# Sums for a blocked matrix product, shared out anew between GpSimd and VectorE: attention, then a bilinear feed-forward layer, on one Trainium2 core

## The chip, the cores and the metric

The kernel runs on one core of one Trainium2 chip. The core has five engines that run at the same time, each with its own queue of instructions: TensorE (PE in the profile; PEld are its weight loads), VectorE (DVE), ScalarE (ACT), GpSimd (POOL) and SyncE (SP, which here only starts DMA transfers). They share a large on-chip memory, SBUF; the results of products land in a smaller one, PSUM, which GpSimd doesn't read here. Semaphores tell an engine that another has done its part. The metric is the device time of one launch, in microseconds (us); less is better.

## What is computed

Four batches of 8 heads, 768 positions and 64 numbers a head go through block attention: a small 8 x 8 matrix P per head, normalized by rows and columns five times, mixes the 8 blocks of k and v, and each block of q attends to its mixed block. The result, as x with 3072 rows of 512, goes through a feed-forward layer that multiplies two projections by each other.

```python
def _attn_ref(q, k, v, sort_net):
    ...
    k_sorted = np.einsum('bhij,bhjcd->bhicd', P, k_b).reshape(B, H, S, D)
    v_sorted = np.einsum('bhij,bhjcd->bhicd', P, v_b).reshape(B, H, S, D)
    ...
    scores = scale * np.matmul(q_b, k_sb.transpose(0, 1, 2, 4, 3))
    ...
    return np.matmul(attn, v_sb).reshape(B, H, S, D).astype(np.float32)

def _moe_ref(x, w_a, w_b, w_out):        # x: 3072 x 512
    a = x @ w_a                          # w_a, w_b: 512 x 1536
    b = x @ w_b
    return (a * b @ w_out).astype(np.float32)   # w_out: 1536 x 512
```

## The kernel before, in words

Everything is computed in bf16 with fp32 sums. The work goes batch by batch: while TensorE runs the feed-forward layer of batch b, the attention of batch b + 1 is put between its steps. The order on every engine is written out by hand: `interleave` (L697) runs a list of feed-forward steps and, after the step numbers given in `places`, the units of the next batch's attention. Each engine takes its instructions strictly in that order.

**Attention units** (`units_full`, L672). For pair g of heads: M mixes the blocks of k and v on TensorE and ScalarE copies them out; R computes the scores (`pair_scores`, L326) into tiles `sc` in PSUM, and ScalarE takes their exponent; O (`pair_o` and `one_o`, L341 and L273) multiplies by v into tiles `o_ps`, and VectorE divides by the sums (`rec` at L282, `xp` at L284). The tiles `mix`, `sc` and `o_ps` come from one pool of two PSUM buffers (`psA`): a new one waits until the one before last has been read. Then DMA transposes on SP's queue bring x to its place (`xT`). M also has GpSimd's share: for pairs 5 and 7 it spreads P over a tile `s_all` (L167, one half of the heads of a later batch each time), and regroups q and k, v (`pair_q`, `regroup`). On GpSimd's queue lie the loads of later pairs too, with a one-element copy `held` (L295) ahead of some of them, which waits until x of an earlier pair has landed.

**Feed-forward steps.** `ffn_ab` (L391) computes one block of 128 columns of a and of b for half of the 768 rows: 4 products of 384 columns each into a tile `pf` of a pool of four PSUM buffers (`psF`). ScalarE copies a out (L403), and VectorE multiplies it with b straight from PSUM (L404) into `hT`, the product h. When the columns of h that belong together are done, sums of them are due.

**Why there are sums.** The products with w_out (`ffn_out_pair`, L491), and in batch 3 those with w_a (`ab_four`, L592), treat rows and columns as 2 x 2 blocks and need seven block products instead of eight, but sums and differences of blocks as operands. There are four kinds:

- `weight_sum` (L451): five sums `w_sums[n]` of blocks of w_out, each in two pieces of 128 x 768, made once;
- `h_sums` (L460): for each block of columns m, one sum of two parts (768 elements), one of one part (384) and a difference in place (768);
- `a_sum` (L558) and `x_sum` (L573): the same for w_a and for x, for batch 3 alone.

Sums that are due stand in the list `sums_due`; `some_sums(n)` (L383) puts the next n of them on VectorE's queue, after a step of `ffn_ab`, in `ffn_out` and in `ab_four`; `sums_for` (L387) puts those there that a product is about to need. The ten pieces of `weight_sum` become due in the eighth step of batch 0's second half (L853), when the loads of w_out (L127) have been started.

**The outputs of batch 0.** For the first third of the columns, `ffn_out` (L422) uses plain products, for c = 0 and then c = 3, each in two parts with `some_sums(2)` after each; the rest goes through `ffn_out_pair` in four parts: parts 1 and 2 need the w_sums n = 1, 2 and 0, and parts 3 and 4 need n = 4 and 3. The units of batch 1's attention stand between these parts.

**Batch 3** (`ab_four`). One row m of it makes four blocks of h: 7 block products of two matmuls each for a, 4 products of four matmuls each for b, 30 matmuls of 384 columns in all. ScalarE copies two of the products out (L622, L624), and GpSimd adds them to y (L625); VectorE adds a third (L628). The blocks h(1, 0) and h(0, 1) come from `middle` (ScalarE's copy of a, L618) times `kept_b` (ScalarE's copy of b to SBUF, L613), multiplied on GpSimd (L632, L636). The corners h(0, 0) and h(1, 1) take y less a product (L642), and VectorE multiplies them with b from PSUM (L645). Six rows follow each other, then the w_out products of batch 3 and the last stores. The x sums of batch 3 are made on VectorE after the last two parts of batch 2's outputs (L884, L885).

Of the kernel before, what the change touches and what calls it, by code (L numbers as in the profile page):

```python
# [9 lines left out]
FP32 = mybir.dt.float32  # L10
# [3 lines left out]
ALU = mybir.AluOpType  # L14
# [9 lines left out]
def kernel(  # L24
# [11 lines left out]
    nc = tc.nc  # L36
    P = 128
# [14 lines left out]
    KH = KO // 2  # L52
# [8 lines left out]
    HW = S // 2  # L61
# [6 lines left out]
    ld = ctx.enter_context(tc.tile_pool(name="ld", bufs=4))  # L68
# [311 lines left out]
    sums_due = []  # L380
    PACE = (1,1,1,1,1,1,1,2,2,2,2,3)

    def some_sums(n):  # L383
        for _ in range(min(n, len(sums_due))):
            sums_due.pop(0)[1]()
# [36 lines left out]
    def ffn_out(b, c):  # L422
        v = {}

        def mms(ms):
            for m in ms:
                nc.tensor.matmul(v["po"], lhsT=hTs[b][:, m, c * P:(c + 1) * P],
                                 rhs=w_out_sb[:, m, :], start=(m == 0), stop=(m == KO - 1))

        def part1():  # L430
            v["po"] = psF.tile([P, DMODEL], FP32, tag="F", name="po")
            mms(range(KH))
            some_sums(2)

        def part2():
            mms(range(KH, KO))
            o_sb = outp.tile([P, DMODEL], FP32, tag="o2", name="o_sb", bufs=3)
            copy("act", o_sb, v["po"])
            store(b, c, o_sb)
            some_sums(2)  # L440

        return [part1, part2]
# [5 lines left out]
    sums = {}  # L448
    w_sums = [const.tile([P, KH, NH], BF16, name=f"w_sum{n}") for n in range(5)]

    def weight_sum(n, m, nm):  # L451
        x, y = (B11, B12, B21, B11, B21)[n], (B22, B22, B11, B12, B22)[n]
        return n, lambda: nc.vector.tensor_tensor(
            out=w_sums[n][:, m:m + nm], in0=x[:, m:m + nm], in1=y[:, m:m + nm],
            op=ALU.subtract if n in (1, 2) else ALU.add)

    def h_part(b, r, c, m):
        return hTs[b][:, c * KH + m, r * HW:(r + 1) * HW]

    def h_sums(b, m, nm):  # L460
        n0, n = (P, HW - P) if b == 0 else (0, HW)
        if b not in sums:
            sums[b] = ffp.tile([P, KH, 3, HW], BF16, tag="hs", name="hs")
        hT, hs = hTs[b], sums[b]

        def h(r, c, step):
            return _ap(hT, (c * KH + m) * S + r * HW + n0,
                       [[KO * S, P], [S, nm]] + [[step, 2]] * (step is not None) + [[1, n]])

        def s(i, k):  # L470
            return _ap(hs, (m * 3 + i) * HW + n0,
                       [[KH * 3 * HW, P], [3 * HW, nm]] + [[HW, k]] * (k > 1) + [[1, n]])

        turn = KH * S - HW
        return [("h", lambda to=to, x=x, y=y, op=op: nc.vector.tensor_tensor(  # L475
                    out=to, in0=x, in1=y, op=op))
                for to, x, y, op in (
                    (s(0, 2), h(0, 0, 0), h(0, 1, HW), ALU.add),
                    (s(2, 1), h(1, 0, None), h(1, 1, None), ALU.add),
                    (h(1, 0, turn), h(0, 0, KH * S + HW), h(1, 0, turn), ALU.subtract))]  # L480
# [92 lines left out]
    def x_sum(b, n):  # L573
        (r0, c0), (r1, c1) = (((0, 0), (1, 1)), ((0, 0), (0, 1)), ((1, 0), (1, 1)),
                              ((1, 1), (0, 1)), ((0, 0), (1, 0)))[n]
        x_sums[n] = qtp.tile([P, 2, NB, 3 * CG], BF16, tag="qc" if n < 3 else "qTf",
                             name=f"x_sum{n}", bufs=3)
        nc.vector.tensor_tensor(out=x_sums[n], in0=x_part(b, r0, c0), in1=x_part(b, r1, c1),  # L578
                                op=ALU.subtract if n > 2 else ALU.add)
# [12 lines left out]
    def ab_four(b, m):  # L592
        hT = hT_of(b)
        if m < 2:
            spare[m] = ld.tile([P, 2, HW], FP32, tag="kv", name="two_a")
        s2 = spare[m % 2]
        acc = [psA.tile([P, 2, 512], FP32, tag="A", name="acc")[:, 0, 0:HW] for _ in range(2)]
        y = ld.tile([P, HW], FP32, tag="q2", name="y_a")

        def a_tile():  # L600
            return ffp.tile([P, HW], BF16, tag="a_sb", name="a_sb", bufs=4)

        def b_of(c, t):
            pf = psF.tile([P, 512], FP32, tag="F", name="pf")
            ab_mms(pf, w_b_sb, b, m + c * KH, t, range(KA))
            return pf[:, 0:HW]

        def h(c, t):
            return hT[:, m + c * KH, t * HW:(t + 1) * HW]

        def kept_b(c, t):
            b_sb = ld.tile([P, HW], FP32, tag="q2", name="b_sb")
            nc.scalar.copy(out=b_sb, in_=b_of(c, t))  # L613
            return b_sb

        def middle(n):
            a_sb = a_tile()
            nc.scalar.copy(out=a_sb, in_=acc[n])  # L618
            return a_sb

        a_product(acc[0], (b, 0, 0), a_sums[1], m)
        nc.scalar.copy(out=s2[:, 0], in_=acc[0])  # L622
        a_product(acc[1], (b, 1, 1), a_sums[2], m)
        nc.scalar.copy(out=s2[:, 1], in_=acc[1])  # L624
        nc.gpsimd.tensor_tensor(out=y, in0=s2[:, 0], in1=s2[:, 1], op=ALU.add)  # L625
        pf = psF.tile([P, 512], FP32, tag="F", name="pf1")[:, 0:HW]
        a_product(pf, 0, a_sums[0], m)
        nc.vector.tensor_tensor(out=y, in0=pf, in1=y, op=ALU.add)  # L628
        b_sb = kept_b(1, 0)
        a_product(acc[0], 1, C22, m, False)  # L630
        a_sb = middle(0)
        nc.gpsimd.tensor_tensor(out=h(1, 0), in0=a_sb, in1=b_sb, op=ALU.mult)  # L632
        a_product(acc[1], 2, C11, m, False)
        a_sb = middle(1)
        b_sb = kept_b(0, 1)
        nc.gpsimd.tensor_tensor(out=h(0, 1), in0=a_sb, in1=b_sb, op=ALU.mult)  # L636
        some_sums(1)
        corners = []
        for n in range(2):
            a_product(acc[n], 3 + n, a_sums[3 + n], m, False)  # L640
            a_sb = a_tile()
            nc.vector.tensor_tensor(out=a_sb, in0=y, in1=acc[n], op=ALU.subtract)  # L642
            corners.append(a_sb)
        for n in range(2):
            nc.vector.tensor_mul(out=h(n, n), in0=corners[n], in1=b_of(n, n))  # L645
            some_sums(1)
        if m in (1, 3, 4, 5):
            sums_due[:0] = h_sums(b, *((m - 1, 2) if m < 4 else (m, 1)))

# [54 lines left out]
    with tc.manual_schedule(engines={ET.PE, ET.Pool, ET.SP, ET.Activation, ET.DVE}):  # L706
        if True:
# [22 lines left out]
            for it in range(5):  # L730
                rsum, csum = chain[0][it], chain[1][it]
                nc.scalar.activation(out=p_nat, in_=p_nat, func=AF.Exp)
                if it == 2:
                    with nc.allow_low_precision("sum of one one and zeros"):
                        nc.vector.reduce_sum(
                            out=mask, in_=_ap(ident, 0, [[P, P], [1, CG], [CG, NB]]),
# [3 lines left out]
                if it == 4:  # L740
                    pace(rsum, 10)
                nc.vector.tensor_mul(out=p_nat, in0=p_nat,
                                     in1=_ap(rsum, 0, [[NB, BH], [1, NB], [0, NB]]))
# [4 lines left out]
                if it < 4:  # L748
                    nc.vector.tensor_mul(out=p_nat, in0=p_nat,
                                         in1=_ap(csum, 0, [[NB, BH], [0, NB], [1, NB]]))  # L750
                else:
                    nc.vector.tensor_mul(
                        out=p_fin.bitcast(BF16).rearrange("h (i j u) -> h i j u", i=NB, j=NB),
                        in0=_ap(p_nat, 0, [[NB * NB, BH], [NB, NB], [1, NB], [0, 2]]),
                        in1=_ap(csum, 0, [[NB, BH], [0, NB], [1, NB], [0, 2]]))
# [89 lines left out]
        def outs(b):  # L845
# [5 lines left out]
        halves = [n for m in range(KH) for n in (m, m + KH)]  # L851
        steps = [lambda m=m: ffn_ab(0, m, 1) for m in halves]
        steps[7] = lambda m=halves[7]: (  # L853
            sums_due.extend(weight_sum(n, m0, 3) for n in (1, 2, 0, 4, 3) for m0 in range(0, KH, 3)),
            ffn_ab(0, m, 1))
        steps += outs(0)
        interleave(steps, units_full(1), (1, 2, 4, 5, 7, 9, 10, 12, 13, 15, 16, 18))
# [1 line left out]
        def after(step, more):  # L859
            def both():  # L860
                step()
                more()
            return both

        for b in range(1, B):
            ab = {}

            def ab_begun(m, t, b=b, ab=ab):
                if b == 1 and m == t == 0:
                    for key in ((0, w_a_sb), (0, w_b_sb)):  # L870
                        pf = psF.tile([P, 512], FP32, tag="F", name="pf")
                        ab.setdefault(key[0], []).append(pf)
                        ab_mms(pf, key[1], b, 0, key[0], range(KA - 1))
                return ab.get(t, ()) if m == 0 else ()

            steps = [lambda m=m, t=t, b=b: ffn_ab(b, m, t, ab_begun(m, t))
                     for m in halves for t in range(2)]
            if b == B - 1:
                steps = [lambda m=m, b=b: ab_four(b, m) for m in range(KH)]
            steps += outs(b)  # L880
            if b == 2:
                steps[1] = after(steps[1], lambda: sums_due.extend(
                    a_sum(n, kc) for n in (2, 3, 0, 1, 4) for kc in range(2)))
                steps[-2] = after(steps[-2], lambda: (x_sum(3, 0), x_sum(3, 1)))  # L884
                steps[-1] = after(steps[-1], lambda: (x_sum(3, 2), x_sum(3, 3), x_sum(3, 4)))  # L885
            interleave(steps, units_full(b + 1) if b + 1 < B else [],
                       (1, 4, 8, 10, 13, 15, 17, 20, 21, 24, 25, 28))

# [29 lines left out]
```

## Time and profile before

| What | us |
|---|---|
| median of 3 runs (233.94 to 234.71) | 233.94 |
| the profiled execution, its own time | 233.79 |
| its span, first to last instruction | 232.0 |
| TensorE busy | 225.8 |
| VectorE busy | 158.4 |
| ScalarE busy | 120.9 |
| GpSimd busy | 87.7 |
| w_out: three loads started | 38.9 to 40.4 |
| outputs of batch 0 on TensorE | 62.6 to 79.5 |
| batch 3's rows on TensorE | 183.2 to 214.1 |

All places in the trace are microseconds from the start of the span. The median time of a launch is a little above the span, since a launch has a start and an end outside of it. A group of instructions has one line: its line in the kernel, engine, operation, what it writes and reads, its shape and how often; then its busy time and the mean of one in ns. A line of the order of time has start, duration, engine, line and operation, and in brackets how long the engine sat idle before it and what ended that. A line of the busy time by stage has the stretch, its length and the busy time of each engine in it with the number of instructions in brackets, then the granted TensorE clock, and the DMA share and rate.

### The profile page before, as it was taken

The page shows a single profiled execution, that of the slowest core. Times are in us where ns is not written, and L with a number is a line of the kernel's source. Part 1 is how long each engine was busy: PE and PEld are TensorE (multiplying, and loading weights), DVE is VectorE, ACT ScalarE, POOL GpSimd, SP SyncE. Part 2 cuts the span into 40 slices and gives each one's busy share as a digit, 9 for nine tenths or more (in the row PEclk, how much of TensorE's full clock was granted, in tenths as well). Part 3 has the DMA queues.
Part 4 walks back from the last instruction along what each step waited for, and adds up shares of the span by engine and source line. Part 5 has one row for each costly group of instructions (what it writes and reads, how often), then busy time and mean ns, then how long its engine had stood idle before and what let it go on. Part 6 is the DMA issues. An engine that isn't in the chain of part 4 may idle for free.

```text
span 232.0 us, 5823 instructions
## 1 busy us (share of the span) xinstructions
PE 225.8 (97%) x2281; PEld 158.9 (68%) x2283; DVE 158.4 (68%) x352; ACT 120.9 (52%) x260; POOL 87.7 (38%) x116
## 2 busy tenths in 40 slices
PE   7999999999999999999999999999999989999994
PEld 7876766766549865666689865666698745555783
DVE  7776777446999334758886347778785675979732
ACT  3575854687633375655552375656543445544231
POOL 8779839840041555237622010000000156766000
PEclk9999999999999999999999999999999999999999
DMA  5999999999759999998999454224025300000042
GB/s 71 201 201 199 206 204 199 196 196 157 133 86 213 144 201 170 165 186 110 132 179 209 158 127 79 42 41 82 12 47 155 132 34 0 1 0 3 2 168 104
DMA packets 54859, 28.70 MB, mean 124 GB/s; under 512 B 33712, under 2 KB 51888, under 8 KB 54832
## 3 DMA queue, kind: packets, MB, share of 16 engines
q0 software_dynamic: 18832, 14.16, 44.8%
q1 hardware_dynamic: 35856, 14.04, 31.7%
q8 instruction: 18, 0.29, 0.5%
q10 hardware_dynamic: 144, 0.13, 0.2%
q14 instruction: 9, 0.07, 0.1%
HBM read 28.32 MB, written 6.29 MB: 149 GB/s over the span
## 4 chain that ended last, share of the span: by engine, by line
PE 86%; DVE 7%; issue 2%; DMA 2%; ACT 1%; POOL 0%; POOLq 0%; DVEq 0%
PE pf L372 44%; PE po L484 21%; PE mix L312 3%; PE o_ps L278 3%; PE acc L588 3%; DMA first<-in_q_dram 2%; PE sc L333 2%; PE heat L181 1%; DVE x_sum L578 1%; DVE hT L475 1%; PE mixh L224 1%; PE sc L237 1%; DVE hs L475 1%; PE xt_ps L269 1%; PE q_ps L202 1%
## 5 line engine op out<-in xcount | busy, mean ns | idle before, releaser
L372 PE MATMUL pf<-xT,w_b_sb 128*128 128x384 bf16 x384 | 77.9, 326 | 0.0
L404 DVE TENSOR_TENSOR hT<-a_sb,pf 128x384 bf16<-128x384 bf16 x72 | 39.7, 552 | 38.1 <-ACT a_sb L403 22.9
L372 PE MATMUL pf<-xT,w_a_sb 128*128 128x384 bf16 x280 | 57.5, 326 | 0.0
L372 PEld LDWEIGHTS <-w_b_sb 128*128 128x128 bf16 x384 | 37.5, 98 | 24.9
L403 ACT CAST a_sb<-pf 128x384 bf16<-128x384 f32 x70 | 34.0, 486 | 33.7 <-PE pf L372 28.7
L372 PEld LDWEIGHTS <-w_a_sb 128*128 128x128 bf16 x288 | 25.9, 98 | 14.3
L484 PE MATMUL po<-w_sum,hT 128*128 128x256 bf16 x264 | 31.9, 273 | 0.3 <-DVE hT L645 0.3
L625 POOL TENSOR_TENSOR y_a<-two_a 128x384 f32<-128x384 f32 x6 | 6.0, 1005 | 58.5 <-ACT two_a L624 58.5
L484 PEld LDWEIGHTS <-hT 128*128 128x128 bf16 x264 | 25.4, 98 | 3.9 <-DVE hT L645 0.7
L175 ACT CAST kv<-mix 128x384 bf16<-128x384 f32 x48 | 19.5, 493 | 4.7 <-PE mix L312 4.6
L338 ACT ACTIVATE eT<-sc 96x768 bf16<-96x768 f32 x24 | 18.1, 802 | 6.0 <-PE sc L333 6.0
L484 PEld LDWEIGHTS <-hs 128*128 128x128 bf16 x198 | 19.1, 98 | 2.5 <-DVE hs L475 0.4
L475 DVE TENSOR_TENSOR hs<-hT 128x768 bf16<-128x768 bf16 (+5 forms) x32 | 20.4, 652 | 0.4
L505 DVE TENSOR_TENSOR o<-y,po 128x256 f32<-128x256 f32 x22 | 9.2, 420 | 11.9 <-PE po L484 11.9
L498 ACT COPY s<-po 128x256 f32<-128x256 f32 x22 | 8.0, 374 | 17.8 <-PE po L484 17.8
L284 DVE TENSOR_TENSOR xp<-o_ps,rec 96x512 bf16<-96x512 f32 x24 | 16.5, 687 | 0.8
L484 PE MATMUL po<-w_out_sb,hs 128*128 128x256 bf16 x132 | 16.4, 273 | 0.0
L111 POOL COPY kvc<-kv 128x768 uint32<-128x768 uint32 x16 | 13.3, 843 | 7.5 <-PE mix L312 7.2
L498 ACT COPY o<-po 128x256 f32<-128x256 f32 x22 | 8.2, 372 | 15.0 <-PE po L484 15.0
L299 POOL COPY qc<-q 128x384 uint32<-128x384 uint32 x12 | 6.4, 535 | 23.3 <-DMA q<-in_q_dram 18.3
L100 POOL DMA_DIRECT2D kv<-in_k_dram x16 | 11.6, 724 | 3.0 <-PE o_ps L278 2.1
L475 DVE TENSOR_TENSOR hT<-hT 128x1536 bf16<-128x1536 bf16 (+3 forms) x16 | 12.6, 786 | 0.1
(99 smaller groups left out, 303.1 us busy)
## 6 DMA issues: line engine op xcount, KB each, us to landing
out_dram<-o SPq DMA_DIRECT2D x17, 256.0 KB, 2.4
kv<-in_k_dram POOLq DMA_DIRECT2D x16, 192.0 KB, 7.6
kv<-in_v_dram POOLq DMA_DIRECT2D x16, 192.0 KB, 8.0
q<-in_q_dram POOLq DMA_DIRECT2D x12, 192.0 KB, 8.4
w_out_sb<-in_moe_w_out_dram POOLq DMA_DIRECT2D x3, 512.0 KB, 12.4
out_dram<-o SPq DMA_DIRECT2D x9, 128.0 KB, 6.7
w_a_sb<-in_moe_w_a_dram POOLq DMA_DIRECT2D x2, 512.0 KB, 11.0
w_b_sb<-in_moe_w_b_dram POOLq DMA_DIRECT2D x2, 512.0 KB, 12.6
```

What stands on the lines that cost most here:

```text
L100: nc.gpsimd.dma_start(out=to, in_=_ap(t, base, [[W, P], [S * D, 2], [1, W]]))
L111: nc.gpsimd.tensor_copy(out=to.bitcast(U32).rearrange("p c n d -> p n c d"), in_=loaded[g][0].bitcast(U32).rearrange("p n (c d) -> p n c d ...
L175: nc.scalar.copy(out=out, in_=in_)
L284: nc.vector.tensor_tensor(out=_ap(xp, i0 * 2 * D, [[nxp * 2 * D, BLK], [D, 2], [2 * D, NBH], [1, D]]), in0=_ap(o_ps, 1, [[1024, BLK], [511 ...
L338: nc.scalar.activation(out=eT[:, hf, :, 0:HB], in_=sc[0:BLK, :, 0:HB], func=AF.Exp, scale=float(scale))
L372: nc.tensor.matmul(pf[:, 0:HW], lhsT=w_sb[:, kc, m * P:(m + 1) * P], rhs=x_cols(b, kc, t), start=(kc == 0), stop=(kc == KA - 1))
L403: nc.scalar.copy(out=a_sb, in_=pf[:, 0:HW])
L404: nc.vector.tensor_mul(out=hT[:, m, t * HW:(t + 1) * HW], in0=a_sb, in1=ab[1][:, 0:HW])
L475: return [("h", lambda to=to, x=x, y=y, op=op: nc.vector.tensor_tensor(out=to, in0=x, in1=y, op=op)) for to, x, y, op in ((s(0, 2), h(0, 0 ...
L484: nc.tensor.matmul(to, lhsT=lhs(m)[:, u * P:(u + 1) * P], rhs=rhs[:, m], start=start and m == 0, stop=(m == KH - 1), skip_group_check=not ...
L498: nc.scalar.copy(out=to, in_=v["ps"][n])
L505: nc.vector.tensor_tensor(out=to, in0=v["y"], in1=v["ps"][n], op=ALU.subtract)
```

## The change

The diff does five things.

- `weight_sum` and `h_sums` take an engine as argument.
- Of the ten pieces of the w_out sums, the four of n = 4 and n = 3 go straight onto GpSimd's queue in the eighth step of batch 0's second half; the six others stay in the list for VectorE. `ffn_out` asks for no sums after its first part for c = 0.
- In batch 3, y and the two products that GpSimd made go to VectorE, which reads b from PSUM; `kept_b` goes away, and with it two copies a row on ScalarE.
- In batch 3, the sums of h of rows 0 to 4 go onto GpSimd's queue at the end of their row, one row at a time; those of row 5 stay on VectorE.
- The five x sums move one part ahead each: two, two and one after the last three parts of batch 2's outputs.

In the list of instructions that results, GpSimd's four pieces stand behind the last `regroup` before them and ahead of the spread of P for batch 3 and of the first `held` copy with its loads.

```diff
@@ ffn_out
         def part1():
             v["po"] = psF.tile([P, DMODEL], FP32, tag="F", name="po")
             mms(range(KH))
-            some_sums(2)
+            some_sums(2 if c else 0)
...
-    def weight_sum(n, m, nm):
+    def weight_sum(n, m, nm, eng=nc.vector):
         x, y = (B11, B12, B21, B11, B21)[n], (B22, B22, B11, B12, B22)[n]
-        return n, lambda: nc.vector.tensor_tensor(
+        return n, lambda: eng.tensor_tensor(
...
-    def h_sums(b, m, nm):
+    def h_sums(b, m, nm, eng=nc.vector):
...
-        return [("h", lambda to=to, x=x, y=y, op=op: nc.vector.tensor_tensor(
+        return [("h", lambda to=to, x=x, y=y, op=op: eng.tensor_tensor(
                     out=to, in0=x, in1=y, op=op))
@@ ab_four
-        def kept_b(c, t):
-            b_sb = ld.tile([P, HW], FP32, tag="q2", name="b_sb")
-            nc.scalar.copy(out=b_sb, in_=b_of(c, t))
-            return b_sb
...
-        nc.gpsimd.tensor_tensor(out=y, in0=s2[:, 0], in1=s2[:, 1], op=ALU.add)
+        nc.vector.tensor_tensor(out=y, in0=s2[:, 0], in1=s2[:, 1], op=ALU.add)
         pf = psF.tile([P, 512], FP32, tag="F", name="pf1")[:, 0:HW]
         a_product(pf, 0, a_sums[0], m)
         nc.vector.tensor_tensor(out=y, in0=pf, in1=y, op=ALU.add)
-        b_sb = kept_b(1, 0)
+        pf = b_of(1, 0)
         a_product(acc[0], 1, C22, m, False)
-        a_sb = middle(0)
-        nc.gpsimd.tensor_tensor(out=h(1, 0), in0=a_sb, in1=b_sb, op=ALU.mult)
+        nc.vector.tensor_mul(out=h(1, 0), in0=middle(0), in1=pf)
         a_product(acc[1], 2, C11, m, False)
         a_sb = middle(1)
-        b_sb = kept_b(0, 1)
-        nc.gpsimd.tensor_tensor(out=h(0, 1), in0=a_sb, in1=b_sb, op=ALU.mult)
-        some_sums(1)
+        nc.vector.tensor_mul(out=h(0, 1), in0=a_sb, in1=b_of(0, 1))
...
         for n in range(2):
             nc.vector.tensor_mul(out=h(n, n), in0=corners[n], in1=b_of(n, n))
-            some_sums(1)
-        if m in (1, 3, 4, 5):
-            sums_due[:0] = h_sums(b, *((m - 1, 2) if m < 4 else (m, 1)))
+        if m < KH - 1:
+            for _, run in h_sums(b, m, 1, nc.gpsimd):
+                run()
+        else:
+            sums_due[:0] = h_sums(b, m, 1)
...
         steps[7] = lambda m=halves[7]: (
-            sums_due.extend(weight_sum(n, m0, 3) for n in (1, 2, 0, 4, 3) for m0 in range(0, KH, 3)),
+            sums_due.extend(weight_sum(n, m0, 3) for n in (1, 2, 0) for m0 in range(0, KH, 3)),
+            [weight_sum(n, m0, 3, nc.gpsimd)[1]() for n in (4, 3) for m0 in range(0, KH, 3)],
             ffn_ab(0, m, 1))
...
-                steps[-2] = after(steps[-2], lambda: (x_sum(3, 0), x_sum(3, 1)))
-                steps[-1] = after(steps[-1], lambda: (x_sum(3, 2), x_sum(3, 3), x_sum(3, 4)))
+                for n, of in ((-3, (0, 1)), (-2, (2, 3)), (-1, (4,))):
+                    steps[n] = after(steps[n], lambda of=of: [x_sum(3, i) for i in of])
```

## Prediction

> **What bounds the kernel now.** I read the busy shares first, then the busy time by stage, then the order of time of VectorE (DVE) and GpSimd (POOL), then single groups.
>
> ```profile
> PE 225.8 (97%) x2281; PEld 158.9 (68%) x2283; DVE 158.4 (68%) x352; ACT 120.9 (52%) x260; POOL 87.7 (38%) x116
> 56.00:60.00 4.00, 4.00 (x48) 2.87 (x46) 3.67 (x7) 2.53 (x7) 0.00 (x0) 1.00 1.00 126
> 60.00:64.00 4.00, 3.93 (x36) 2.09 (x36) 3.92 (x10) 2.46 (x4) 0.00 (x0) 1.00 0.65 116
> 64.00:68.00 4.00, 3.64 (x45) 1.89 (x43) 3.86 (x11) 1.08 (x2) 2.06 (x4) 1.00 0.36 58
> 68.00:72.00 4.00, 3.95 (x49) 3.00 (x45) 3.93 (x10) 2.35 (x5) 0.27 (x1) 1.00 1.24 145
> ...
> 182.00:190.00 8.00, 7.31 (x49) 4.45 (x48) 7.04 (x12) 3.30 (x8) 3.23 (x3) 1.00 0.19 69
> ```
>
> TensorE (PE) works for 97% of the span, so the end moves by what it waits. Columns are length, then PE, weight loads, DVE, ACT, POOL. From 56 to 72 us VectorE has 15.4 of 16 us filled and GpSimd is nearly idle; TensorE loses 0.5. In batch 3 it loses about 0.7 at the start.
>
> Two things decide what moved work costs: how GpSimd and VectorE share, and when w_out is there.
>
> ```profile
> 76.69 0.52 POOL L299 COPY qc<-q 128x384 uint32<-128x384 uint32 x1
> 77.14 1.03 POOL L111 COPY kvc<-kv 128x768 uint32<-128x768 uint32 x1
> 76.89 0.60 DVE L522 TENSOR_TENSOR y<-s 128x256 f32<-128x256 f32 x1 [1.29 <-ACT s L498]
> ...
> 196.78 0.92 POOL L632 TENSOR_TENSOR hT<-a_sb,b_sb 128x384 bf16<-128x384 bf16 x1 [0.36 <-ACT a_sb L618]
> 196.93 1.58 DVE L475 TENSOR_TENSOR hs<-hT 128x1536 bf16<-128x1536 bf16 x1
> 197.70 1.59 POOL L636 TENSOR_TENSOR hT<-a_sb,b_sb 128x384 bf16<-128x384 bf16 x1
> ...
> 192.54 1.02 DVE L642 TENSOR_TENSOR a_sb<-y_a,acc 128x384 bf16<-128x384 f32 x2 [0.29 <-PE acc L588]
> 192.82 0.92 POOL L636 TENSOR_TENSOR hT<-a_sb,b_sb 128x384 bf16<-128x384 bf16 x1
> ```
>
> L522 reads two SBUF tensors; alone it takes 0.42. Here it ends at 77.49, 0.28 after GpSimd's copy ended (77.21): it was held, all but 0.14 of start-up, then ran. The next copy took 1.03 for 0.83: held until 77.49. At 196.93 the sum waits for L632 (197.70), and L636, next in line, then takes 1.59 for 0.92: it waits for the sum. So they take turns, one whole instruction at a time. L642, with one operand in PSUM, keeps its 0.5 beside L636: it needs no turn.
>
> ```profile
> L167 POOL TENSOR_TENSOR s_all<-mask,p_col 128x1024 bf16<-128x1024 bf16 x3 | 6.1, 2019 | 0.0
> L167 POOL TENSOR_TENSOR s_all<-mask,p_col 128x512 bf16<-128x512 bf16 x1 | 1.1, 1105 | 0.0
> L453 DVE TENSOR_TENSOR w_sum<-w_out_sb 128x768 bf16<-128x768 bf16 x10 | 5.0, 549 | 0.0
> L127 POOL DMA_DIRECT2D w_out_sb<-in_moe_w_out_dram x3: 750/760/762, 38.9 to 40.4; - x3
> DMA to landing us min/median/max: 9.8/12.4/14.9
> ```
>
> GpSimd's two-input bf16 work costs 1.105 for 512 and 2.0 for 1024 elements, so 1.555 for 768 and, 1.76 ns an element down, 0.88 for 384. VectorE needs 0.549 for 768. The last part of w_out lands at 40.4 + 14.9 = 55.3.
>
> **Part one: four pieces of w_out sums on GpSimd.** They (4 x 1.555) start when w_out is whole, at 55.4, and the 2.0 us spread now stands behind them. That is just where VectorE is full. In the new order of instructions VectorE still meets five two-input sums there, each holding its queue for one GpSimd turn. Ends, new against old: sum of h (1024) 57.48 against 57.36; sum (512), behind piece two (58.90), 59.17 against 57.69; difference (1024), behind piece three (60.59), 61.14 against 58.76; its own w_out sum, behind piece four (62.55), 62.96 against 59.23; sum (512), behind the spread (64.82), 65.10 against 60.43. (A GpSimd turn begins when VectorE's ends and, 0.14 of start-up saved, adds 1.42, or 1.86 for the spread.) VectorE is 4.7 us late. Behind it stand L404, which empties the PSUM that pf needs, and the x tiles of L284, which empty what the scores (L333) need: those go from 62.0 to 66.2 and the next eight from 62.4 to 67.0, +4.7 on TensorE's path.
>
> Back comes 0.6: the first part of ffn_out takes no sums, so two pieces (2 x 0.47) no longer stand ahead of the next L282 and L284, for which TensorE waited 0.42 and 0.36 at 67.1 to 67.8, about 0.8 less 0.2 of new wait; the four taken off VectorE (1.9) had cover, as TensorE was not waiting at 70. Sum **+4.1**, first product of batch 1 from 79.5 to 83.6. Nothing regains it: from 80 to 182 TensorE shows no idle time to give up.
>
> At nothing: the spread (heads of batch 3, mixed at 132) and the held copies and loads behind it on POOL's queue. The spread ends at 64.8; the hold behind it waits for x, at 65.9 before and some 4.7 later now. Were it late, the load (landed 73.4) has 3.3 us until its copy at 76.7. SP keeps its order.
>
> **Part two: x sums a step sooner.** Three of them ran behind GpSimd's y and products, 3.0 us for 3 x 0.47. Now four lie in the 1.3 us waits of VectorE ahead of L505, and no GpSimd work is beside them. The first row of batch 3 takes 5.86 from first product to first product (183.23 to 189.09) against 30 products x 0.1625 = 4.87: **-1.0**. x is there (last transpose issued 175.9, landed 178.7, first sum at 181.5).
>
> **Part three: batch 3's rows.** ACT drops 12 copies (0.48 each); it is half idle, so nothing. VectorE has eight operations a row, 0.47 apart, under 4.87: it would fit alone. But y now reads two SBUF tensors, and GpSimd runs 768 + 384 + 768 of h sums (4.0) in each of the next five rows. Who is first? GpSimd starts 0.08 after the last product of a row (L637 of the new kernel). y needs ACT's copy of acc, and acc needs the second corner read: that ends 0.92 before the row's last product, and 0.06 + 0.49 (two products) + 0.07 + 0.48 (copy) + 0.06 = 1.16 later y may start, 0.24 after that product. GpSimd is first each time. The loop: 0.08 + 1.555 + 0.41 (y after its turn) + 0.58 (L623) + 6 x 0.463 = **5.41 a row**, over TensorE's 4.87; before, rows 2 to 6 took 4.87 to 5.07. The last product comes 5.63 + 5 x 5.41 = 32.7 after the first of the batch; before, 215.78 - 183.23 = 32.55. After it the sums of row 5 come first on VectorE (before, a 0.55 rest of row 4 did): -0.15. So parts two and three together: 0.0.
>
> Sum against the profiled execution: 233.79 (span 232.0 and 1.8 around it) + 4.1 = 237.9. The median shown, 233.94, is 0.15 above that execution: **238.0**.
>
> **Unknown cost.** No row has this sum on GpSimd. Below, the copy of 768 (L111, 0.83, one input); above, twice L632 (2 x 0.92 = 1.84). I take the spreads' 1.555, same type and two inputs. Three pieces are waited for in full: 0.83 makes part one 4.1 - 3 x 0.725 = 1.9, and a loop of 4.69, under 4.87, frees batch 3 of its waits: 1.65 us in the rows (183.23 to 214.12 against 6 x 4.875) and 0.8 in what follows (14.56 us of w_out products against 126 x 0.1092), -2.4; sum 233.5. 1.84 gives +0.9 and 5 x 0.285 = 1.4: 240.3. Between 1.4 and 1.7 a piece: 236.8 to 239.2.
>
> The Trainium skill, GPSIMD Engine Reference, Engine selection, holds GpSimd about 2x slower than VectorE for two-input elementwise work. The row says 1.555 / 0.549 = 2.8; by the page's ratio a piece would take 1.1 and the sum be 4.1 - 3 x 0.455 - 2.4 + 5 x 0.08 = 0.7, so 234.7; by the row it is 238.0. The rule speaks against the change in either case.
>
> **Rivals.**
> - No turns: GpSimd's sums run beside VectorE's. Then 0.4 at 67 us and 2.45 in batch 3 are gained: 231.1. For it: both engines have idle time in the averages. Against: the three rows at 76.9 and 196.9. Chance 0.05.
> - Not slower: GpSimd is quick on dense rows, under some 0.97 us a piece (there part one's +2.4 meets batch 3's -2.4). At a copy's 0.83, 233.5. For it: the copies. Against: L632 takes 0.92 for half as many. Chance 0.06.
> - The clock falls too. The forecast has TensorE idle for 2.0 us twice (61.5 to 63.5, 64.3 to 66.2). In the last 2 us of the span the granted clock is 0.88, so it fell 2 to 2.5 us after the last product. Estimate: half speed for 4 to 5 us there, 2 to 2.5 us: 240.3. Against: no wait so far, 1.1 us at most, lowered it. Chance 0.13.
>
> The Trainium skill, TensorE: Matmul & The Clock Gate, Part 1, wants about a 3.4 us window idle before the clock halves: by it nothing, 238.0; by the row perhaps 2.5.
>
> **How the numbers follow.** The forecast has 0.76, time 238.0, own range 236.8 to 239.2. The low rivals hold 0.11 and stay outside, most of the clock's case goes in: 236.0 to 240.5. Less than 0.5% (1.2 us) can't be told from no change. Faster: 0.05 (no turns). Same: 0.06 (quick GpSimd). Slower: 0.76 + 0.13 = 0.89.
>
> **What would show it.** TensorE idle for some 4 us between 60 and 70 us, VectorE's L475 and L453 there stretched to 1.5 to 2 us, one after each GpSimd piece of 1.5; scores at 66; batch 1 from 83.6; no x sum wait; y (L620) at 1.3 to 1.9 us in rows 2 to 6, rows of 5.4. Pieces under 1.0, or unstretched sums, prove it wrong.

## The result, and the profile after

The changed kernel takes 243.09 us (median of 4 runs, 242.09 to 244.33) against 233.94 before: a ratio of 1.0388, interval 1.0329 to 1.0447. The forecast of 238.0 us had the direction and, as the experiments show, the mechanism of each part that it summed, but it left the fall of the TensorE clock out of the sum: it is 5 us short, and the time lies above its range of 236.0 to 240.5.

The profiled execution is the longest of the four, 244.33 us with a span of 242.6. Its busy shares first, then the busy time by stage at the places shown of before (length, then TensorE, weight loads, VectorE, ScalarE, GpSimd, then the granted clock).

```profile
PE 228.2 (94%) x2283; PEld 159.1 (66%) x2283; DVE 168.5 (69%) x357; ACT 116.0 (48%) x248; POOL 98.8 (41%) x117
```

```profile
56.00:60.00 4.00, 4.00 (x34) 2.69 (x33) 2.65 (x3) 3.15 (x8) 1.81 (x1) 1.00 1.60 154
60.00:64.00 4.00, 2.65 (x30) 1.66 (x28) 4.00 (x4) 1.58 (x4) 4.00 (x4) 1.00 0.84 164
64.00:68.00 4.00, 0.95 (x4) 0.29 (x3) 3.97 (x4) 0.00 (x0) 3.96 (x2) 0.67 0.42 65
68.00:72.00 4.00, 2.67 (x21) 1.22 (x22) 3.90 (x11) 1.61 (x2) 0.00 (x0) 0.50 0.25 47
72.00:76.00 4.00, 4.00 (x26) 2.05 (x25) 3.03 (x8) 0.00 (x0) 2.32 (x4) 0.55 0.51 67
```

TensorE, idle for 0.5 us from 60 to 72 before, is now idle for 5.7 (12.00 - 2.65 - 0.95 - 2.67). VectorE is busy all the time there and does a handful of instructions. And the granted clock, the column after GpSimd, which stood at 1.00 in all these stages before, falls to 0.50: what work TensorE has from 65 to 76 us it does at half speed.

The order of time shows who waits for whom (start, duration, engine, line; in brackets idle time before and what ended it).

```profile
60.76 1.66 DVE L475 TENSOR_TENSOR hT<-hT 128x1024 bf16<-128x1024 bf16 x1
62.34 1.98 DVE L453 TENSOR_TENSOR w_sum<-w_out_sb 128x768 bf16<-128x768 bf16 x1
64.82 3.28 DVE L475 TENSOR_TENSOR hs<-hT 128x512 bf16<-128x512 bf16 x2
...
58.19 7.62 POOL L453 TENSOR_TENSOR w_sum<-w_out_sb 128x768 bf16<-128x768 bf16 x4 [9.07 <-DMA w_out_sb<-in_moe_w_out_dram]
65.78 2.18 POOL L167 TENSOR_TENSOR s_all<-mask,p_col 128x1024 bf16<-128x1024 bf16 x1
72.64 0.18 POOL L295 COPY held<-xT 1x1 bf16<-1x1 bf16 x1 [4.69 <-DMA xT<-xp]
...
64.84 0.95 PE L372 MATMUL pf<-xT,w_b_sb 128*128 128x384 bf16 x4 [2.18 <-DVE hT L404]
69.00 0.50 PE L333 MATMUL sc<-qTf,kv 64*128 64x96 bf16 x8 [3.21 <-DVE xp L284]
69.83 0.50 PE L333 MATMUL sc<-qTf,kv 64*128 64x96 bf16 x8 [0.33 <-DVE xp L284]
...
204.18 2.83 POOL L475 TENSOR_TENSOR hs<-hT 128x768 bf16<-128x768 bf16 x2 [1.03 <-DVE hT L637]
204.26 1.98 DVE L620 TENSOR_TENSOR y_a<-two_a 128x384 f32<-128x384 f32 x1 [0.16 <-ACT two_a L619]
```

A difference of 1024 elements takes VectorE 1.66 us for 0.69, its own w_out sum 1.98 for 0.55, two sums of h 3.28 for 0.63: each lies behind one GpSimd piece or the spread. TensorE waits 2.18 us for the multiplication L404 and 3.21 for the x tiles of L284, the two the forecast named. The hold on GpSimd waits 4.69 us for x, so GpSimd's queue delays nothing. In batch 3 GpSimd's sum starts 0.08 us before y, and y takes 1.98 us.

The groups give the lengths (busy time, then the mean of one in ns):

```profile
L475 POOL TENSOR_TENSOR hT<-hT 128x768 bf16<-128x768 bf16 x5 | 8.2, 1638 | 0.4
L475 POOL TENSOR_TENSOR hs<-hT 128x768 bf16<-128x768 bf16 x5 | 8.2, 1636 | 58.6 <-PE acc L588 54.5 <-DVE hT L637 4.1
L453 POOL TENSOR_TENSOR w_sum<-w_out_sb 128x768 bf16<-128x768 bf16 x4 | 7.6, 1934 | 9.1 <-DMA w_out_sb<-in_moe_w_out_dram 9.1
L620 DVE TENSOR_TENSOR y_a<-two_a 128x384 f32<-128x384 f32 x6 | 9.9, 1644 | 1.3 <-ACT two_a L619 1.3
```

GpSimd's sum of 768 takes 1.64 us where VectorE leaves it alone, 0.08 over the forecast's 1.555; the w_out pieces take 1.93, with their waits.

Set against the profile of before instruction by instruction, TensorE's offset (how much later in its span it starts the same instruction) grows as follows: +1.24 by 17 us (the second load of the start-up landed 1.1 us later in this execution), +7.5 at the scores, +9.67 at batch 1, +8.69 after the x sums, +10.8 at the first w_out products of batch 3, +10.5 at the end.

### The profile page after: what moved, and what is told of

The parts are those of the page before. It is cut to its first block, busy times and chain, and to the rows that moved or that the text cites. A ratio compares the mean times of both kernels' runs of the same rounds, so it can differ in the third digit from the quotient of the medians.

```text
span 242.6 us, 5808 instructions
## 1 busy us (share of the span) xinstructions
PE 228.2 (94%) x2283; PEld 159.1 (66%) x2283; DVE 168.5 (69%) x357; ACT 116.0 (48%) x248; POOL 98.8 (41%) x117
## 4 chain that ended last, share of the span: by engine, by line
PE 84%; DVE 6%; DMA 4%; POOL 3%; issue 2%; ACT 0%; POOLq 0%
PE pf L372 42%; PE po L484 21%; PE acc L588 5%; DMA kv<-in_k_dram 4%; PE o_ps L278 3%; PE mix L312 3%; PE po L427 3%; PE sc L333 2%; POOL kv L100 2%; DVE hs L475 1%; DVE hT L629 1%; PE pf L588 1%; DVE a_sb L634 1%; PE xt_ps L269 1%; DVE w_sum L453 1%
## 5 line engine op out<-in xcount | busy, mean ns | idle before, releaser
L404 DVE TENSOR_TENSOR hT<-a_sb,pf 128x384 bf16<-128x384 bf16 x72 | 39.7, 552 | 38.3 <-ACT a_sb L403 23.1
L475 POOL TENSOR_TENSOR hs<-hT 128x768 bf16<-128x768 bf16 (+1 forms) x10 | 14.1, 1431 | 58.6 <-PE acc L588 54.5
L111 POOL COPY kvc<-kv 128x768 uint32<-128x768 uint32 x16 | 14.1, 892 | 10.4 <-PE mix L312 10.3
L475 DVE TENSOR_TENSOR hs<-hT 128x768 bf16<-128x768 bf16 (+5 forms) x26 | 18.0, 711 | 0.4
L284 DVE TENSOR_TENSOR xp<-o_ps,rec 96x512 bf16<-96x512 f32 x24 | 16.5, 687 | 0.8
L100 POOL DMA_DIRECT2D kv<-in_v_dram x16 | 11.5, 719 | 3.1 <-DMA first<-in_q_dram 1.6
```

Source lines behind the costliest of these rows:

```text
L100: nc.gpsimd.dma_start(out=to, in_=_ap(t, base, [[W, P], [S * D, 2], [1, W]]))
L111: nc.gpsimd.tensor_copy(out=to.bitcast(U32).rearrange("p c n d -> p n c d"), in_=loaded[g][0].bitcast(U32).rearrange("p n (c d) -> p n c d ...
L284: nc.vector.tensor_tensor(out=_ap(xp, i0 * 2 * D, [[nxp * 2 * D, BLK], [D, 2], [2 * D, NBH], [1, D]]), in0=_ap(o_ps, 1, [[1024, BLK], [511 ...
L404: nc.vector.tensor_mul(out=hT[:, m, t * HW:(t + 1) * HW], in0=a_sb, in1=ab[1][:, 0:HW])
L475: return [("h", lambda to=to, x=x, y=y, op=op: eng.tensor_tensor(out=to, in0=x, in1=y, op=op)) for to, x, y, op in ((s(0, 2), h(0, 0, 0), ...
```

## The experiments

Four questions: does each part cost what was forecast (batch 3 alone, part one alone); what does the clock cost (TensorE kept busy); who is first in the turns (short first, n = 3 first, two pieces); and where do the 1.3 us come from that the sum of the parts lacks. Every ratio is against runs of the kernel before on the same chip (its medians there: 233.9 to 235.0).

**Batch 3 alone.** The changed kernel with part one undone.

```diff
-            some_sums(2 if c else 0)
+            some_sums(2)
...
-            sums_due.extend(weight_sum(n, m0, 3) for n in (1, 2, 0) for m0 in range(0, KH, 3)),
-            [weight_sum(n, m0, 3, nc.gpsimd)[1]() for n in (4, 3) for m0 in range(0, KH, 3)],
+            sums_due.extend(weight_sum(n, m0, 3) for n in (1, 2, 0, 4, 3) for m0 in range(0, KH, 3)),
```

> The changed kernel with the w_out part undone: all ten pieces of w_out sums back in VectorE's list and two sums after the first part of the plain outputs; batch 3's part of the change stays. My theory (the time goes where GpSimd's four pieces make VectorE wait, 56 to 78 us): TensorE's first w_out product pair and batch 1 start where they did before (79.5 us, give or take 1.2 us of start-up), x sums give 1.0 us, rows 2 to 6 of batch 3 take 5.58 us, 234.5 us in all, clock 1.0 throughout. Rival (batch 3's rows are where most of it goes): 238 or more.

Measured 234.93 us (234.64 to 235.99), ratio 1.0038 [1.0016, 1.0059]. TensorE lies where it lay before up to batch 3; the x sums gain 0.97 us (offset -0.07 to -1.04), the rows give back 2.1 (to +1.06). The gain of the x sums was as forecast; the loop from one row's sums on GpSimd to the next takes 5.575 us in place of 5.41.

**Part one alone.** The kernel before with the four pieces on GpSimd (`weight_sum` takes an engine, as in the change) and no sums asked for in the first part of `ffn_out` for c = 0.

```diff
-            some_sums(2)
+            some_sums(2 if c else 0)
...
-            sums_due.extend(weight_sum(n, m0, 3) for n in (1, 2, 0, 4, 3) for m0 in range(0, KH, 3)),
+            sums_due.extend(weight_sum(n, m0, 3) for n in (1, 2, 0) for m0 in range(0, KH, 3)),
+            [weight_sum(n, m0, 3, nc.gpsimd)[1]() for n in (4, 3) for m0 in range(0, KH, 3)],
```

> The kernel before with the w_out part alone: four pieces of w_out sums on GpSimd, no sums after the first part of the plain outputs for c = 0; batch 3 as before. My theory: the scores of batch 1's third pair come 6 us late, the granted clock halves for some 10 us from about 65 us, batch 1 starts 8.4 us later than before; 242.3 us. Rival (the pieces cost only their waits, without the clock): 238 to 239.

Measured 240.8 us (240.42 to 242.79), ratio 1.0306 [1.0258, 1.0353]. Batch 1 starts 6.6 us later than before, not 8.4: w_out landed at 55.7 us here, and the half clock lasted 6.83 us. The product of the two ratios, 1.0038 x 1.0306 = 1.0345, lies inside the interval of the whole change.

**Kept busy.** The changed kernel, with products of 128 columns whose results nobody reads in TensorE's two waits (34 in the first, 50 in the second).

```diff
+            if (b, m, t) == (0, KO - 1, 1):
+                for _ in range((34, 50)[n]):
+                    nc.tensor.matmul(pf[:, HW:512], lhsT=warm[:, 0:P], rhs=warm[:, 0:P],
+                                     start=True, stop=True)
```

> The changed kernel, with 34 products of 128 columns on data of zeros after the last a product of batch 0's h and 50 after the last b product, into unused columns of the same PSUM tiles: 1.9 and 2.8 us of TensorE work laid into the two long waits. The outputs stay as they were. Theory (the wait of VectorE costs some 5 us and the halved clock some 3.5 more): the clock stays at 1.0, the scores come as late as in the changed kernel (within 0.5 us), batch 1 starts 3 to 3.5 us earlier; 239.7 us. Rival (the clock fell in a stretch in which VectorE sets the pace anyway, and costs nothing): 243 us.

Measured 240.11 us (239.48 to 241.7), ratio 1.0282 [1.0237, 1.0326]. The busy time by stage, first of part one alone, then of the kept-busy run:

```profile
60.00:64.00 4.00, 1.65 (x10) 0.78 (x8) 4.00 (x4) 0.96 (x2) 4.00 (x3) 1.00 0.68 120
64.00:68.00 4.00, 1.74 (x18) 0.79 (x19) 3.90 (x8) 0.50 (x1) 1.58 (x1) 0.59 0.03 4
68.00:72.00 4.00, 3.78 (x31) 2.00 (x27) 3.04 (x9) 1.11 (x2) 1.40 (x3) 0.56 0.26 49
```

```profile
60.00:64.00 4.00, 3.41 (x43) 2.71 (x42) 3.97 (x4) 0.96 (x2) 4.00 (x3) 1.00 0.56 96
64.00:68.00 4.00, 3.99 (x71) 3.55 (x70) 3.93 (x8) 0.07 (x1) 1.35 (x1) 1.00 0.02 4
68.00:72.00 4.00, 3.95 (x36) 2.10 (x34) 3.86 (x11) 2.02 (x3) 1.58 (x3) 1.00 0.26 49
```

The clock column stays at 1.00. VectorE is as full as without the fills and the scores come at the same offset (+5.35; part one alone +5.48), so the waits are untouched; batch 1 starts 4.82 us late in place of 6.62. The waits alone cost 4.8 us, and the half clock, of 6.83 us, costs 1.8 more (one traced execution of each). The median, 240.11, is inside the forecast's range: what else the sum had wrong wouldn't have carried it out.

**Half kept busy.** The same, with the first fill alone: `range((34, 0)[n])`.

> The changed kernel with only the first of the two fills of the kept-busy run: 34 products of 128 columns in the wait at 62 us, nothing in the wait at 66 us. Theory (the clock is granted stretch by stretch of 3.41 us, and half speed follows a stretch with less than some 1.5 us of full-speed work in it): the stretch with the first wait now holds enough, the one with the second wait doesn't, so the clock falls once, one stretch later than in the changed kernel (from about 68 us) and for 3.41 us only; batch 1 some 5.5 to 6.5 us later than before, time 0.7 to 1.5 us above the kept-busy run, 240.8 to 241.6 us. Rival (it is the first wait that lowers the clock): no fall, 240.1 us as with both fills. Rival (any wait of over 3 us lowers it for as long as before): 6.83 us or more at half clock, 241.8 us or more.

Measured 243.85 us (242.27 to 244.46), ratio 1.0397 [1.0337, 1.0456]: as slow as the change. Start-up and w_out were late in its profiled execution (1.1 us late, and 56.9 against its own start), so the time can't weigh the clock; the clock's place can. First the changed kernel, then this one, by stretches of 3.41 us laid on the moment at which the clock changed.

```profile
58.55:61.96 3.41, 3.41 (x40) 2.35 (x38) 3.41 (x4) 2.49 (x6) 3.41 (x3) 1.00 1.44 152
61.96:65.37 3.41, 1.23 (x9) 0.58 (x6) 3.38 (x4) 0.48 (x1) 3.41 (x2) 1.00 0.67 117
65.37:68.79 3.42, 0.41 (x2) 0.00 (x0) 3.39 (x4) 0.00 (x0) 2.58 (x2) 0.50 0.24 37
68.79:72.20 3.41, 2.87 (x21) 1.32 (x22) 3.31 (x10) 1.61 (x2) 0.00 (x0) 0.50 0.31 58
72.20:75.61 3.41, 3.41 (x23) 1.79 (x22) 2.48 (x6) 0.00 (x0) 2.32 (x4) 0.50 0.44 57
```

```profile
60.46:63.87 3.41, 3.41 (x44) 2.63 (x41) 3.41 (x3) 0.53 (x2) 3.41 (x3) 1.00 0.91 171
63.87:67.28 3.41, 1.38 (x15) 0.74 (x12) 3.38 (x4) 0.48 (x1) 3.41 (x2) 1.00 0.50 77
67.28:70.70 3.42, 1.48 (x17) 0.85 (x19) 3.35 (x8) 1.24 (x2) 0.57 (x1) 0.50 0.00 0
70.70:74.11 3.41, 3.19 (x23) 1.76 (x23) 2.45 (x7) 0.38 (x1) 0.33 (x2) 0.50 0.81 62
```

Half speed follows a stretch with little TensorE work: after 1.23 us of 3.41 in the changed kernel; here that stretch is filled, 3.41 of 3.41, and the fall comes after the next one with 1.38. So the fall went one stretch on, as expected, and the rival that only the first wait lowers the clock is out. The duration was missed: two stretches in place of one in this execution, where the second wait reached over the boundary. Of the other three, two have the mean granted clock of one stretch (0.993, as in the two-piece run below) and one that of two (0.985). All four times lie above the 240.8 to 241.6 expected, those two included (242.27 and 244.46), which is not explained.

**Short first.** The changed kernel; in batch 3 GpSimd does the sum of one part (384) ahead of that of two (768).

```diff
-            for _, run in h_sums(b, m, 1, nc.gpsimd):
+            two, one, turned = [run for _, run in h_sums(b, m, 1, nc.gpsimd)]
+            for run in (one, two, turned):
                 run()
```

> The changed kernel with GpSimd's three sums of a row in another order: the one of 384 elements first. Theory (y loses its turn to the first sum of the row before, each time; the loop is 0.08 + sum + 0.41 + 0.58 + 2.78): with a first sum of 0.91 us instead of 1.64 the loop is 4.8 us, under TensorE's 4.87; rows take 4.87 to 4.95 instead of 5.58 and the end of the batch has no wait, 3.0 us less than the changed kernel, 240.1 us. Rival (GpSimd's total of 4.2 us a row is what counts, or VectorE's eight operations): rows stay at 5.5, 243 us.

Measured 238.03 us (237.85 to 240.09), ratio 1.019 [1.0143, 1.0237]. Groups of this run:

```profile
L620 DVE TENSOR_TENSOR y_a<-two_a 128x384 f32<-128x384 f32 x6 | 5.1, 849 | 2.5 <-ACT two_a L619 2.5
L475 POOL TENSOR_TENSOR hs<-hT 128x384 bf16<-128x384 bf16 x5 | 4.5, 909 | 56.1 <-PE acc L588 54.5 <-DVE hT L637 1.6
```

y waits for 0.91 us of GpSimd work at most, and takes 0.85 in the mean for 1.64. The rows fall to 4.87 us, TensorE's own, and batch 3 ends 2.4 us sooner against its start than before. What made its rows slow is who comes first, not that the sums are on GpSimd. Batch 1 starts 6.4 us late, close to part one alone; the time is 2.1 us under the 240.1 expected, which was reckoned from the change's time; in the change's profile batch 1 starts 9.67 late.

**Short first, w_out sums on VectorE.** Both edits above: part one undone, short one first.

> The changed kernel with all w_out sums on VectorE as before, and the h sums of batch 3 on GpSimd with the short one (384 elements) first, so that y finds GpSimd's turn short. Theory (the order of GpSimd's turns decides whether batch 3 gains): rows of about 4.87 to 4.9 us, no stage of batch 0 disturbed, batch 3 2.4 us shorter than before, time 231.6 us (231.2 to 232.0). Rival (the gain of the short-first order was in part recovered loss of the late batch 0, or the rows stay above 5.0): 233 us or more.

Measured 231.4 us (231.25 to 232.67), ratio 0.988 [0.984, 0.991]: as expected, and the fastest of all. This version beats both kernels. Its rows take 4.87 us, and batch 3 is 2.5 us shorter than before. The profiled execution is the longest of the six, 232.67: batch 0 isn't quite undisturbed in it, since TensorE waits 1.27 us for x at 81.9 us, which it didn't before.

**The same without the two early sums** (`some_sums(2 if c else 0)` kept).

> The run before this, and in addition the first part of ffn_out takes no sums for c = 0. Theory (the two pieces that stand ahead of L282 and L284 are what TensorE waits for at 67 to 68 us, 0.42 and 0.36): 0.4 less, 231.2 us (230.9 to 231.5). Rival (the two pieces must be made anyway and the next product waits for them instead): the same 231.6, or up to 0.5 more.

Measured 233.21 us (231.83 to 237.99), ratio 0.992 [0.988, 0.995]: longer in the median than either expectation, though five of the twelve executions lie at 231.8 to 232.0. In the traced one (233.35 us) the scores after the two sums do come 0.5 us sooner, and at 75 and 80 us TensorE loses 1.06 and 1.33. TensorE's waits there, first in the run before this one, then in this one:

```profile
81.88 0.32 PE L372 MATMUL pf<-xT,w_a_sb 128*128 128x384 bf16 x1 [1.27 <-DMA xT<-xp]
```

```profile
74.87 2.26 PE L484 MATMUL po<-w_sum,hT 128*128 128x256 bf16 x18 [0.76 <-DVE w_sum L453]
82.56 0.32 PE L372 MATMUL pf<-xT,w_a_sb 128*128 128x384 bf16 x1 [1.09 <-DMA xT<-xp]
```

The first loss is the rival's mechanism: a product waits for the sums that were put off. The second is there in the run before as well, with the two early sums kept. Here the copy that holds back the next loads took 2.4 us (66.98 to 69.36), there 0.18, so this loss isn't put down to the copy.

**Two pieces.** The kernel before with n = 3 on GpSimd and n = 4 on VectorE, no early sums.

```diff
-            some_sums(2)
+            some_sums(2 if c else 0)
...
-            sums_due.extend(weight_sum(n, m0, 3) for n in (1, 2, 0, 4, 3) for m0 in range(0, KH, 3)),
+            sums_due.extend(weight_sum(n, m0, 3) for n in (1, 2, 0, 4) for m0 in range(0, KH, 3)),
+            [weight_sum(n, m0, 3, nc.gpsimd)[1]() for n in (3,) for m0 in range(0, KH, 3)],
```

> The kernel before with only two of the four pieces (n = 3) on GpSimd, n = 4 on VectorE; ffn_out's first part takes no sums for c = 0. Theory (each piece on GpSimd holds VectorE for one turn): scores 2.5 us later, batch 1 2.3 later, too short a wait for the clock to fall, time 236.2 us; if the clock falls all the same, 1.8 more, 238.0. Rival (the spread alone, put behind anything, is what makes VectorE late, and not the pieces): 238.5 us or more. Rival (cost in proportion to the pieces, clock and all): 237.2 us.

Measured 238.81 us as the median of four: three at 238.8 to 239.0 with a mean granted clock of 0.993, and one at 234.38 with 1.00, too far apart for a ratio. One of the 17 executions of the kernel before beside them took 240.02 at 0.993 as well. What follows is the traced one, 239.01. All three expectations had the place wrong. n = 3 reads only the first half of w_out, which is there by 52.9; its pieces run at 49.4 and 52.9, and the scores come on time (offset -0.01). The loss is at 79 to 88 us: two waits for x, and then half clock.

```profile
66.67 2.53 POOL L295 COPY held<-xT 1x1 bf16<-1x1 bf16 x1 [9.69 <-DMA xT<-xp]
69.14 0.76 POOL L100 DMA_DIRECT2D kv<-in_k_dram  x1
...
71.32 0.42 POOL L295 COPY held<-xT 1x1 bf16<-1x1 bf16 x1
71.69 0.72 POOL L100 DMA_DIRECT2D kv<-in_k_dram  x1
...
66.73 2.89 DVE L453 TENSOR_TENSOR w_sum<-w_out_sb 128x768 bf16<-128x768 bf16 x6
...
81.75 0.32 PE L372 MATMUL pf<-xT,w_a_sb 128*128 128x384 bf16 x1 [2.24 <-DMA xT<-xp]
84.10 0.32 PE L372 MATMUL pf<-xT,w_a_sb 128*128 128x384 bf16 x1 [1.53 <-DMA xT<-xp]
```

```profile
77.88:81.30 3.42, 1.63 (x14) 1.21 (x13) 0.84 (x2) 0.37 (x1) 1.27 (x2) 1.00 1.30 193
81.30:84.71 3.41, 1.42 (x12) 0.86 (x12) 0.00 (x0) 0.25 (x1) 0.26 (x2) 1.00 1.21 174
84.71:88.12 3.41, 3.41 (x19) 2.03 (x17) 0.55 (x1) 2.33 (x6) 3.35 (x5) 0.50 1.07 255
```

Without the two early sums, a row of six VectorE sums starts just when x lands (66.73), and the one-element copy behind which the next loads wait takes 2.53 us for 0.18. Its loads go out 3 us later, the next ones right behind them (69.14 to 73.83; before, 66.08 and 74.55), and the x transposes go out among them: the third, issued at 71.58, lands at 81.71; before, 3.6 us were enough. Of the offset of +5.2 that batch 1 keeps, 3.6 is there when the clock falls, and the stretch of half clock adds 1.6.

**Two pieces, early sums kept.** One line: `some_sums(2)` again.

> The two-piece kernel, but ffn_out's first part takes two sums again as before. Theory (in the two-piece run the scores were on time; its loss came at 80 to 84 us, because the held copy on GpSimd was kept waiting 2.5 us by six VectorE sums in a row, the loads behind it bunched, and the x transposes queued behind them): the held copy takes 0.2 us again, no loss at 80 to 84, time that of before, 233.7 to 235.0 as that varies. Rival (moving the two pieces makes the loss by itself): 238.8 us again.

Measured 234.58 us (233.73 to 236.71), ratio 1.0005 [0.9975, 1.0035]: no change against before.

```profile
65.83 1.02 DVE L453 TENSOR_TENSOR w_sum<-w_out_sb 128x768 bf16<-128x768 bf16 x2
67.56 0.18 POOL L295 COPY held<-xT 1x1 bf16<-1x1 bf16 x1 [9.71 <-DMA xT<-xp]
68.45 1.95 DVE L453 TENSOR_TENSOR w_sum<-w_out_sb 128x768 bf16<-128x768 bf16 x4
...
81.64 0.32 PE L372 MATMUL pf<-xT,w_a_sb 128*128 128x384 bf16 x1 [0.18 <-DMA xT<-xp]
```

The copy takes 0.18 us again and the wait for x is 0.18, and none of the twelve executions is near 238.8. So the pieces by themselves don't make the loss. That the late loads do fits the two traces, but it isn't shown: in the run without the early sums above, the copy took as long, the loads stood as close and the same transpose took 9.1 us, yet TensorE waited 1.09 us for x and the clock stayed up; and one of the four executions of two pieces, at 234.38, didn't have the loss (it has no trace).

**n = 3 first.** Part one alone, with `for n in (3, 4)` for `(4, 3)` on GpSimd.

> Part one alone, but with the pieces of n = 3 ahead of those of n = 4 on GpSimd. n = 3 reads the first half of w_out, which lands by 52.1; only n = 4 needs the last load (55.3 or later). Theory (VectorE pays one turn for each GpSimd sum that falls between 55 and 65 us, so two fewer): batch 1's first product 2.3 us later than before in place of 6.6, 236.2 us if the clock stays full, 238.0 if it falls for 6.8 us. Rival (the cost is that of four pieces and a spread, in whatever order): 240.5 us again.

Measured 238.36 us (237.12 to 239.36), ratio 1.0179 [1.0129, 1.023], against 1.0306. The order of the pieces decides some two fifths of part one's cost: n = 3's run at 49.85 and 53.11, and only two stand in the full stretch.

```profile
60.98 0.81 PE L372 MATMUL pf<-xT,w_b_sb 128*128 128x384 bf16 x4 [0.81 <-DVE hT L404]
63.86 0.81 PE L372 MATMUL pf<-xT,w_b_sb 128*128 128x384 bf16 x4 [1.42 <-DVE hT L404]
65.36 0.34 PE L333 MATMUL sc<-qTf,kv 64*128 64x96 bf16 x8 [0.69 <-DVE xp L284]
66.20 0.34 PE L333 MATMUL sc<-qTf,kv 64*128 64x96 bf16 x8 [0.49 <-DVE xp L284]
```

The waits are short and spread out, and the clock stayed at 1.00 in this execution (237.12 us, batch 1 +3.3 for the 2.3 expected, with w_out landing at 56.4). In the other three the mean was 0.992 to 0.993, as one stretch of half clock gives, and the time longer.

**Both.** The 231.4 us kernel with n = 3's pieces on GpSimd as well.

> The short-first run with the two pieces of n = 3 on GpSimd as well, asked for as before. Theory: they run from 49 to 54.6 us where VectorE has gaps, cost nothing and gain nothing, since TensorE doesn't wait for the w_out sums: the same 231.4 us, within 0.3. Rival: the spread behind them meets the sum of h at 56.7 and makes the scores late, 232 us or more.

Measured 232.21 us (231.5 to 233.63), ratio 0.990 [0.987, 0.994]. Nothing gained. The theory and its rival are both in the profile: w_out's second load landed 1.7 us later than before, 0.3 of it start-up (n = 3's second piece could start at 53.87 only), the spread behind it met the sums of h, and the scores were 0.5 us late.

**The change again.**

> The changed kernel again, beside the others on this chip. Theory (its time above the sum of its two parts came of w_out landing later and of a longer stretch at half clock in that execution): about 241.8 us, first product of batch 1 some 6.6 later than before when w_out is whole at 55.6 and the half clock lasts 6.83 us, and 243 or more only in an execution where it lasts 10.24 us. Rival (the two parts together cost more than each alone): 243 us again, with a half clock of 6.83 us.

Measured 243.01 us (241.85 to 243.19), ratio 1.0348 [1.0305, 1.039], equal to the product of the two parts, 1.0345. Its profile (243.17 us, normal start-up) has w_out landing at 57.0, scores 6.4 late, half clock for 10.24 us, batch 1 8.5 late. Where w_out landed at 55.5 to 55.7 (part one alone, kept busy, short first), the scores were 5.4 late and, without fills, the half clock lasted 6.83 us. So this execution was as the theory says. The others weren't: the median didn't come down to 241.8, and one took 243.19 us at a mean clock of 0.986, which is that of 6.83 us at half speed (part one alone has it too), as the rival says. What made that one long isn't known; it has no trace.

## Why the prediction was wrong: the turns as forecast, the clock left out of the sum

- **Turns.** Right. Each VectorE sum of the stretch was held by one GpSimd instruction, y in batch 3 likewise. The rival without turns is out.
- **Which TensorE work waits.** Right: L404's consumer and the scores, and nothing regained from 80 to 182 us. POOL's queue cost nothing, as reckoned.
- **Part one, +4.1.** Measured 4.8 with the clock held up. The term was small by 3 x 0.085 for pieces of 1.64 us and by 0.2 for w_out, which landed at 55.5 in that run: 0.45 of the 0.7. Of the 5.4 that the scores were late, 0.5 came back; the forecast said 0.6.
- **x sums, -1.0.** Measured -0.97.
- **Batch 3's rows, 5.41.** Measured 5.575. The loop lacked two things: 0.085 for the longer piece, and 0.085 because the last product of a row must end in full (0.55) before GpSimd's next sum may start, while the forecast gave it the 0.463 from start to start. Over five loops 0.8: parts two and three together came to +0.9 (ratio 1.0038) in place of 0.0.
- **The clock: the step that failed.** The forecast put "the clock falls too" apart as a rival with 0.13, since "no wait so far, 1.1 us at most, lowered it", and took two idle times of 2.0 us one by one; so the clock stood in the sum at nothing. The runs show that it falls in every traced execution with the four pieces in the change's order, later where the first wait is filled and not at all only where both are, and what counts is the work in a stretch of 3.41 us, where both waits add to the same or neighbouring stretches. Price 1.8 us at 6.83 us of half speed; the rival's estimate was 2 to 2.5 at 4 to 5 us. Half speed costs less than half of its length here, since TensorE waits for VectorE in part of it. (The row that the rival went by has the clock fall at 231.53, 2.7 us after the last product ended at 228.85, and not 2 to 2.5.)
- **The rest.** 4.8 + 1.8 + 0.9 gives 241.4 us. In both profiled executions of the change w_out landed 1.3 us later than in part one alone, measured from the start of the work, which made the scores 0.8 later, and the half clock lasted a stretch more, some 1.0: these account for their 243.2, and the start-up of 1.24 for the 244.3. Why w_out lands anywhere from 55.3 to 57.2 after the start-up is taken off, with nothing changed in the queues ahead of its loads, isn't settled. The other six executions of the change have no trace; their mean clocks of 0.984 to 0.986 tell of 6.83 us at half speed, not 10.24, and they took 241.85 to 243.66, so what lies above 241.4 in them stays open. The forecast took its one landing, 55.3, which is the earliest of all that were seen.

## What to carry to other kernels

Moving elementwise work from a full engine to an idle one can lose time where the two take turns at their operands; look at which instruction is next in turn, because the same sums cost 0.8 us or gained 2.4 by their order alone. Price a stall of TensorE together with what it does to the clock, by all the idle time in some 3.4 us and not by the longest gap. And an instruction that only guards a load is on the path of everything behind that load: here a one-element copy that waited 2.3 us longer went with a loss of some 5 us in one traced execution, though with one of 1.1 in another.

## What the runs showed of the hardware

- **The clock falls without a long gap.** Changes lie 3.41, 6.83 or 10.24 us apart. Half speed followed stretches of 3.41 us with 0.92, 1.23, 1.38 and 1.42 us of TensorE work at full speed (part one alone, the change, half kept busy, two pieces); full speed followed 1.63 and 2.00 (two pieces, n = 3 first). In stretches at half speed, 0.41 to 2.87 us of busy time was followed by another half stretch, 3.19 and 3.20 by full speed; halved, as work at full speed, that is up to 1.44 and from 1.60. One bound, between 1.44 and 1.60 us of full-speed work in a stretch, fits all of these; it is inferred from these traces. The longest single gap doesn't decide: in the two-piece run a stretch whose longest idle piece was 1.8 us kept full speed, and the next, with 1.5 at most, lost it. The Trainium skill, TensorE: Matmul & The Clock Gate, Part 1, tells of a free-running window of 3413 ns, which these lengths agree with; it speaks of an idle window, and here a window with 1.42 us of work was enough.
- **Turns aren't kept for a one-element copy.** Sums of 768 on GpSimd came in after each single VectorE sum; the held copy of the two-piece run, begun at 66.67, ended at 69.20, after five VectorE sums in a row, and that of the run without the early sums did the same (66.98 to 69.36). The Trainium skill, SBUF — State Buffer, Who interferes with whom, has the later one block until the first instruction is finished; the row shows five. Why isn't settled.
- **Transposes take longer among bunched loads.** In the two traces with two sets of three loads 0.3 us apart instead of 5 to 7, the third x transpose took 10.1 and 9.1 us from issue to landing; in the twelve others, 2.8 to 5.9.
